# Two cached attentions in decode: aligned ring slots, and one set's query weights dealt to 64 partitions by an indirect DMA

## The chip, the cores and the metric

The kernel runs on one core of one Trainium2 chip. The metric is the device time of one execution in microseconds (us). PE is the matrix engine, DVE the vector engine, ACT the scalar engine, POOL the GpSimd engine, and SP the engine that only issues transfers here. Transfers are carried by 16 DMA engines.

## The reference, cut to what matters

One token attends to two caches of 8192 positions, one with 16 key and value heads (A), one with 8 that are shared by two query heads each (B). The two results are mixed by a gate.

```python
x = A_x                                        # [1, 1, 448]
g = sigmoid((x * gate_w).sum(-1))
q_A = (x @ A_wq).reshape(16, 256)              # B: the same, with B_wq
p_A = softmax(q_A . A_k_cache * 256 ** -0.5)   # caches: [16 or 8, 8192, 256], float32
a = (p_A @ A_v_cache).reshape(1, 4096) @ A_wo  # wo: [4096, 448]
return g * a + (1 - g) * b
```

All of it is float32. Each byte of the caches and weights is used once, so 432 MB have to come in.

## The kernel before, in words

The host lays all inputs out as one long array, `stream`, in the order of use. `plan()` cuts it into loads. A load is one `dma_start` on SP's queue: 128 partitions, `FULL` = 15,872 floats in each (63,488 bytes a partition, 8.13 MB in all), written to one of three ring slots (`SLOTS`) in SBUF. 64 loads bring the stream in; the last 13 are smaller, so that work on the last pieces can begin sooner. A load waits until the readers of what lay in its slot are done. While one load is being carried, the next is queued behind it.

There are eight sets (`NS`). A set has one B head that serves two queries and two A heads, each in four tiles of 2048 positions. Its pieces in the stream are query weights (`wq`), keys (`k`), values (`v`) and output weights (`wo`). `piece()` hands each piece to its work: `project` forms the queries of a set from `wq`, one matmul for each of seven columns of 128 input rows (columns 0 to 2 for B, 3 to 5 for A, and one for the rest of both); `spread` puts them where the scores need them; `scores` and `scores_by_row` form the scores of a tile and its probabilities `pr`, on PE and on DVE; `attend` multiplies by the values three tiles later (`LEAD`); `take`, `gather`, `combine`, `column` and `project_o` finish a head; `emit_set` multiplies by the output weights.

A `Recorder` runs `build` twice: the first pass finds which instructions others depend on, the second issues them with semaphore waits. So all instructions but a few have the line of the recorder in the profile: L184 before, L198 in the changed kernel. Tiles are told apart by name. The order of the work on each engine is that of the pieces in the stream.

The first piece of the stream, `xg`, holds the token `x` and the gate's weights; `inputs()` copies `x` into `xz`. In the code before, `xg` does not count against a load's room, so that the first load is 15,880 floats a partition, and a slot is allotted 15,936 (`SLOT`).

Of the kernel before, what the change touches and what calls it, by code (L numbers as in the profile page):

```python
# [3 lines left out]
F32 = mybir.dt.float32  # L4
# [5 lines left out]
P = 128  # L10
D = 448
DH = 256
SK = 8192
NCOL = SK // P
KF = D // P
# [19 lines left out]
TILES = [((s, r), t) for s in range(NS) for r in UNITS for t in range(NT)]  # L35

XG = 2 * (KF + 1)
SLOT = 15936
ATOM = {"half": D, "xg": XG, "k": 2 * DH, "v": 2 * DH, "wq": 2 * DH, "wo": D}  # L40

def plan():

    size = {"xg": XG, "k": ROWS * DH, "v": ROWS * DH, "wq": WQ, "wo": 8 * D}
    per = len(UNITS) * NT
    n = len(TILES)
    items = []
    for i in range(n + LEAD):
        if i == 0:  # L50
            items += [("xg", 0), ("wq", 0)]
        if i < n:
            items.append(("k", i))
        if i >= LEAD:
            items.append(("v", i - LEAD))
        if i % per == 7 and i // per + 1 < NS:
            items.append(("wq", i // per + 1))
        if i % per == LEAD + 1 and i >= per:
            items.append(("wo", i // per - 1))
    loads, room = [[]], FULL  # L60
    last = [("v", n - 3), ("v", n - 2)]
    for kind, i in items[:items.index(last[0])]:
        at, left = 0, size[kind]
        while left:
            step = min(left, room) // ATOM[kind] * ATOM[kind]
            if step:
                loads[-1].append((kind, i, at, step))
            at, left, room = at + step, left - step, room - step * (kind != "xg")
            if left:
                loads.append([])  # L70
                room = FULL

    loads = [[x] for x in loads]
    x = loads[-2][0]
    loads[-2] = [x[:2], x[2:]]
    loads[-1] += [[(kind, i, 0, size[kind])] for kind, i in last]
    at, end = 0, []
    for c in LAST_CUT:
        end.append([("v", n - 1, at, c * DH)])
        at += c * DH  # L80

    for h, n in ((3, 2), (0, 2), (1, 2)):
        end.append([("wo", NS - 1, 2 * h * D, n * D)])
    end += [[("half", c, 0, D)] for c in range(2)]
    return loads + [end]
# [137 lines left out]
        return self.rec.tile(self.name if self.psum else name, shape, dtype, bufs or self.bufs, self.psum)  # L223

def program(nc, stream, out):
    memory = {("slot", i): nc.alloc_sbuf_tensor(f"slot_{i}", [P, SLOT], F32) for i in range(SLOTS)}
    plan = Recorder(nc, memory)
    build(plan, stream, out)
    names = ["tensor", "vector", "scalar", "gpsimd"] + plan.dmas  # L230
    sems = {n: nc.alloc_semaphore(f"{n[0]}{n[1]}" if n[0] == "dma" else n) for n in names}
    rec = Recorder(nc, memory, plan.needed | {(e, plan.count[e] - 1) for e in names[:4]}, sems)
    stores = build(rec, stream, out)
    late = rec.wait("sync", [(e, rec.count[e] - 1) for e in names[:4]] + [d for d in rec.dmas if d not in stores[1:]])
    for sem, value in late:
        nc.sync.wait_ge(sem, value)
    nc.sync.sem_clear(range(sems[names[0]].num, sems[stores[1]].num))
    for d in stores[1:]:
        nc.sync.wait_ge(sems[d], 16)
    nc.sync.sem_clear(range(sems[stores[1]].num, sems[stores[-1]].num + 1))  # L240

def build(nc, stream, out):
    scale = DH ** -0.5

    const = Pool(nc, "const", 1)
# [75 lines left out]
    xz = const.tile([P, KF + 2, BLK], F32, name="xz")  # L322
    nc.vector.memset(xz, 0.0)
    gate = const.tile([1, 2], F32, name="gate")

    def clear(t, n):
        nc.tensor.matmul(t[:, :n], zero, zero[:, None, :n // 4].to_broadcast([P, 4, n // 4]), start=True, stop=False, skip_group_check=True)
# [3 lines left out]

    def inputs(xs):
        nc.vector.tensor_copy(xz[:, :KF, 0], xs[:, :KF])
        nc.vector.tensor_copy(xz[:KR, KF, 0:1], xs[:KR, KF:])
        nc.vector.tensor_copy(xz[KR:, KF + 1, 0:1], xs[KR:, KF:])

    def prepare(gw):
        clear(YY[0], D)
# [12 lines left out]

    def project(s, c0, w):

        if c0 == 0:
            QR[s] = ps_s.tile([2 * BLK, 2 * DH], F32, name="sm")
        q = QR[s]
        for j in range(w.shape[1]):
            a, c = divmod(c0 + j, KF)
            for a in (a,) if a < 2 else (0, 1):
                c = c if c0 + j < 2 * KF else KF  # L360
                nc.tensor.matmul(q[BLK * a:BLK * (a + 1), :], xz[:, c if c < KF else KF + a, :], w[:, j, :],
                                 start=(c == 0), stop=(c == KF), skip_group_check=True)
        if c0 + w.shape[1] == 2 * KF + 1:
            QR[s] = small.tile([P, NB * BLK], F32, name="px")[:2 * BLK, :2 * DH]
            nc.scalar.activation(QR[s], q, AF.Copy)
# [19 lines left out]
    def scores(u, t, j0, kt):  # L385
        M = heads(u)
        if t == 0 and j0 == 0:
            ST[u] = small.tile([P, 2, NT], F32, name="st", bufs=4)
        if j0 == 0:
            SC[u, t] = ps_sc.tile([P, NB * BLK], F32, name="sc")  # L390
        sc = SC[u, t]
        qb = QB[u[0] % 2, u[1]]
        for j in range(kt.shape[1]):
            e, g = divmod(j0 + j, NG)
            at = BLK - R[M] * g - t * M
            nc.tensor.matmul(sc[32 * g:32 * (g + 1), :], qb[:, e, at:at + 32], kt[:, j, :],
                             start=(e == 0), stop=(e == 1), skip_group_check=True)
        if j0 + kt.shape[1] < 2 * NG:
            return
        st = ST[u]  # L400
        mn = small.tile([P, 1], F32, name="mn")
        nc.vector.tensor_reduce(mn, sc, axis=AX.X, op=OP.min)
        nc.vector.tensor_tensor(st[:, 0, t:t + 1], mn, CAP[M][:, t:t + 1], op=OP.min)
        px = small.tile([P, NB * BLK], F32, name="px")
        nc.scalar.activation(px, sc, AF.Exp, bias=st[:, 0, t:t + 1], scale=-1.0, accum_out=st[:, 1, t:t + 1])
        pr = small.tile([P, NB * BLK], F32, name="pr", bufs=LEAD + 2)

        nc.vector.transpose(pr.rearrange("p (q r k) -> p q k r", r=BLK, k=2),
                            px.rearrange("p (q k c) -> p q k c", c=BLK, k=2))
        PR[u, t] = pr.rearrange("p (q c) -> p q c", c=2 * BLK)  # L410

    def scores_by_row(u, t, j0, kt):

        if t == 0 and j0 == 0:
            ST[u] = small.tile([P, 2, NT], F32, name="st", bufs=4)
        st = ST[u]
        n = kt.shape[1]
        nc.vector.tensor_tensor(kt, kt, QA[u][:, None, :].to_broadcast([P, n, DH]), op=OP.mult)
        if j0 == 0:
            SC[u, t] = small.tile([P, ROWS], F32, name="sr")  # L420
        sc = SC[u, t]
        nc.vector.tensor_reduce(sc[:, j0:j0 + n], kt, axis=AX.X, op=OP.add)
        if j0 + n < ROWS:
            return
        mn = small.tile([P, 1], F32, name="mn")
        nc.vector.tensor_reduce(mn, sc, axis=AX.X, op=OP.min)
        mt = small.tile([P, BLK], F32, name="mt")
        nc.vector.transpose(mt, mn.to_broadcast([P, BLK]))
        nc.vector.tensor_reduce(st[:, 0, t:t + 1], mt, axis=AX.X, op=OP.min)
        px = small.tile([P, ROWS // 2, 2], F32, name="pxr")  # L430
        nc.scalar.activation(px.rearrange("p q k -> p (q k)"), sc, AF.Exp, bias=st[:, 0, t:t + 1], scale=-1.0,
                             accum_out=st[:, 1, t:t + 1])
        pr = small.tile([P, NB * BLK], F32, name="pr", bufs=LEAD + 2)[:, :ROWS * NG * NT].rearrange(
            "p (q c k) -> p q c k", c=NG * NT, k=2)
        nc.vector.tensor_tensor(
            pr, px[:, :, None, :].to_broadcast([P, ROWS // 2, NG * NT, 2]),
            cols[:, t].rearrange("p g r -> p (g r)")[:, None, :, None].to_broadcast([P, ROWS // 2, NG * NT, 2]), op=OP.mult)
        PR[u, t] = pr.rearrange("p q c k -> p q (c k)")
# [13 lines left out]
    def take(u):  # L452

        o = O.pop(u)
        ob1 = small.tile([P, DH], F32, name="ob1", bufs=1)
        OB[u] = small.tile([P, DH], F32, name="ob", bufs=3)
        nc.scalar.activation(ob1, o[:, DH:], AF.Copy, scale=half[:, 1:2])
        nc.vector.scalar_tensor_tensor(OB[u], o[:, :DH], half[:, 0:1], ob1, op0=OP.mult, op1=OP.add)

# [14 lines left out]
    def combine(u):  # L474
# [14 lines left out]
        nc.vector.tensor_reduce(z[:, :M], es.rearrange("p (c m) -> p m c", m=M), axis=AX.X, op=OP.add)  # L489
        rz = small.tile([1, 2], F32, name="rz")  # L490
        nc.vector.reciprocal(rz[:, :M], z[:, :M])
        WR[u] = small.tile([1, NG // M, n, M, 2], F32, name=f"wr{M}")
        for m in range(M):
            nc.vector.tensor_scalar(
                WR[u][:, :, :, m, :], ew[:, None, m::M, None].to_broadcast([1, NG // M, n, 2]),
# [83 lines left out]
    def piece(kind, i, at, view):  # L579
        n = view.shape[-1] // ATOM[kind]  # L580
        j0 = at // ATOM[kind]
        if kind == "xg":
            inputs(view[:, :KF + 1])
            GW[0] = view[:, KF + 1:]
        elif kind == "wq":
            project(i, j0, view.rearrange("p (c n) -> p c n", c=n))
            if j0 + n < 2 * KF + 1:
# [39 lines left out]

    off = 0
    for fill in LOADS:
        buf = ring.tile([P, SLOT], F32, name="slot")  # L630
        c = 0
        for load in fill:
            n = sum(x[3] for x in load)
# [76 lines left out]
```

## Time and profile before

| | us |
|---|---|
| median of 3 runs (lowest, highest) | 1009.67 (1009.52, 1009.75) |
| the profiled execution | 1009.6 |
| its span, first to last instruction | 1007.9 |
| PE busy | 579.3 (57%) |
| DVE busy | 458.8 (46%) |
| ACT busy | 94.4 (9%) |
| read from HBM | 432.02 MB, 429 GB/s over the span |
| chain that ended last: share of DMA | 75% |

The times of the steps below come from the one profiled execution. It lies 0.07 us under the median, and 1.7 us of it lie outside the span. In windows of time, the DMA share is the mean busy share of the 16 DMA engines: 0.50 would be eight of them at work. The chain of work follows the end back to whatever released each step.

### The profile page before, as it was taken

The page shows a single profiled execution, that of the slowest core. Times are in us where ns is not written, and L with a number is a line of the kernel's source. Part 1 is how long each engine was busy: PE and PEld are TensorE (multiplying, and loading weights), DVE is VectorE, ACT ScalarE, POOL GpSimd, SP SyncE. Part 2 cuts the span into 40 slices and gives each one's busy share as a digit, 9 for nine tenths or more (in the row PEclk, how much of TensorE's full clock was granted, in tenths as well). Part 3 has the DMA queues.
Part 4 walks back from the last instruction along what each step waited for, and adds up shares of the span by engine and source line. Part 5 has one row for each costly group of instructions (what it writes and reads, how often), then busy time and mean ns, then how long its engine had stood idle before and what let it go on. Part 6 is the DMA issues. An engine that isn't in the chain of part 4 may idle for free.

```text
span 1007.9 us, 7387 instructions
## 1 busy us (share of the span) xinstructions
PE 579.3 (57%) x3154; PEld 170.5 (17%) x3154; DVE 458.8 (46%) x644; ACT 94.4 (9%) x308; POOL 1.9 (0%) x10
## 2 busy tenths in 40 slices
PE   0755745565755655646645475655645637636557
PEld 0211211121211111112111121111211112101112
DVE  1386213961248521576214851248521585215851
ACT  0100100010100110001100000100110101101011
POOL 0000000000000000000000000000000000000000
PEclk9877777767777877787877867876976777777788
DMA  9999999999999999999999999999999999999997
GB/s 403 442 433 421 437 439 434 431 429 434 437 437 423 431 437 438 426 431 434 437 431 434 428 437 431 437 424 438 431 437 431 434 428 437 434 433 421 441 413 328
DMA packets 9256, 432.48 MB, mean 429 GB/s; under 512 B 1032, under 2 KB 1288, under 8 KB 1928
## 3 DMA queue, kind: packets, MB, share of 16 engines
q1 hardware_dynamic: 9220, 432.02, 99.3%
q8 instruction: 24, 0.39, 0.2%
q14 instruction: 8, 0.07, 0.0%
q10 hardware_dynamic: 4, 0.00, 0.0%
HBM read 432.02 MB, written 0.00 MB: 429 GB/s over the span
## 4 chain that ended last, share of the span: by engine, by line
DMA 75%; PE 13%; DVE 11%; ACT 1%; issue 0%; SPq 0%
DMA slot<-in_stream_dram 75%; PE ps_o L184 6%; PE ps_sc L184 5%; DVE sr L184 4%; DVE slot L184 4%; PE ps_s L184 1%; DVE pr L184 1%; DVE mn L184 1%; ACT px L184 0%; PE ps_y L184 0%; ACT pxr L184 0%; DVE st L184 0%; DVE ob L184 0%; ACT ew L184 0%; DVE mt L184 0%
## 5 line engine op out<-in xcount | busy, mean ns | idle before, releaser
L184 PE MATMUL ps_o<-slot,pr 128*32 128x512 f32 (+1 forms) x1536 | 352.0, 760 | 227.2 <-DMA slot<-in_stream_dram 227.2
L184 PE MATMUL ps_sc<-slot,qb 128*32 128x512 f32 x1024 | 195.9, 715 | 105.1 <-DMA slot<-in_stream_dram 105.0
L184 DVE TENSOR_REDUCE mn<-ps_sc 128x1 f32<-128x512 f32 x64 | 44.1, 690 | 338.5 <-PE ps_sc L184 308.3
L184 DVE TENSOR_TENSOR slot<-slot,qa 128x4096 f32<-128x4096 f32 (+7 forms) x40 | 142.6, 3565 | 42.7 <-DMA slot<-in_stream_dram 42.6
L184 PEld LDWEIGHTS ps_o<-slot,pr 128*32 128x32 f32 (+1 forms) x1536 | 80.2, 142 | 408.4 <-DMA slot<-in_stream_dram 255.7
L184 DVE TENSOR_REDUCE sr<-slot 128x16 f32<-128x4096 f32 (+7 forms) x40 | 142.7, 3567 | 1.4
L184 PEld LDWEIGHTS ps_sc<-slot,qb 128*32 128x32 f32 x1024 | 46.6, 130 | 222.9 <-issue 129.4
L184 ACT ACTIVATE px<-ps_sc,st 128x512 f32<-128x512 f32 x64 | 44.0, 688 | 408.2 <-DVE st L184 408.2
L184 DVE STREAM_TRANSPOSE pr<-px 128x512 f32<-128x512 f32 x64 | 45.7, 714 | 54.1 <-ACT px L184 54.1
L184 PE MATMUL ps_s<-slot,xz 128*32 128x512 f32 (+1 forms) x136 | 45.6, 664 | 34.9 <-DVE xz L184 22.9
L184 ACT ACTIVATE pxr<-sr,st 128x16 f32<-128x16 f32 x32 | 9.9, 308 | 372.9 <-DVE st L184 372.9
L184 PE MATMUL ps_s<-sel,ob 128*128 128x1 f32 (+1 forms) x96 | 18.4, 296 | 37.7 <-DVE ob L184 37.7
L184 DVE SCALAR_TENSOR_TENSOR ob<-ps_o,half,ob 128x256 f32<-128x256 f32 x24 | 11.3, 473 | 45.9 <-ACT ob L184 45.9
L184 PEld LDWEIGHTS ps_s<-sel,ob 128*128 128x128 f32 x96 | 16.3, 239 | 62.5 <-DVE ob L184 54.2
L184 PEld LDWEIGHTS ps_s<-slot,xz 128*32 128x32 f32 (+1 forms) x136 | 11.4, 125 | 63.9 <-issue 27.2
L184 DVE TENSOR_TENSOR pr<-pxr,cols 128x256 f32<-128x256 f32 x32 | 13.6, 425 | 15.0 <-ACT pxr L184 15.0
L184 PE MATMUL ps_y<-slot,ocs 128*1 128x448 f32 (+1 forms) x176 | 15.8, 476 | 0.0
L184 ACT ACTIVATE ob<-ps_o,half 128x256 f32<-128x256 f32 x24 | 11.3, 470 | 43.6 <-PE ps_o L184 43.5
L184 PE MATMUL ps_s<-px,spread 64*128 64x256 f32 x16 | 7.1, 532 | 13.9 <-DVE es L184 13.9
L184 PE MATMUL ps_s<-ones,wr 1*128 1x1 f32 x48 | 9.5, 264 | 6.5 <-DVE wr L184 6.5
L184 ACT ACTIVATION_READ_ACCUMULATOR px<-ps_sc,st 128x1 f32 x64 | 12.3, 193 | 0.0
L184 PEld LDWEIGHTS ps_s<-ones,wr 1*128 1x128 f32 x48 | 7.4, 193 | 28.2 <-DVE wr L184 13.3
(62 smaller groups left out, 137.0 us busy)
## 6 DMA issues: line engine op xcount, KB each, us to landing
slot<-in_stream_dram SPq DMA_DIRECT2D x50, 7936.0 KB, 43.0
slot<-in_stream_dram SPq DMA_DIRECT2D x1, 7940.0 KB, 21.8
slot<-in_stream_dram SPq DMA_DIRECT2D x1, 4864.0 KB, 41.4
slot<-in_stream_dram SPq DMA_DIRECT2D x2, 2048.0 KB, 33.3
slot<-in_stream_dram SPq DMA_DIRECT2D x1, 3072.0 KB, 37.8
slot<-in_stream_dram SPq DMA_DIRECT2D x3, 448.0 KB, 33.2
slot<-in_stream_dram SPq DMA_DIRECT2D x1, 1280.0 KB, 31.7
slot<-in_stream_dram SPq DMA_DIRECT2D x1, 1024.0 KB, 32.2
```

Source lines behind the costliest of these rows:

```text
L184: i = getattr(e, what)(*args, **kw)
```

## The change: what it does

Slots are allotted 15,872 floats each behind a tile `pad`, whose length is worked out from the first free byte so that it comes out as a multiple of 256. In the program as built, the first slot began at byte 4224 of a partition before (16 times 256, and 128 over); with the change it begins at byte 1312 (5 times 256, and 32 over), since the pad itself is placed at byte 1152, and a slot is 248 times 256 bytes long.

Columns 0 to 2 of set 2's `wq` (384 rows of 512 floats, 786,432 bytes) leave the stream. The host lays them out as an array `dealt` of 64 rows of 3072 floats (12,288 bytes), each of six of the 384 rows. An indirect DMA, which POOL issues, puts row `row[p]` of it in partition p of a new tile `dq`; for the 64 partitions that get none, `row[p]` is out of bounds and nothing is written. Which partitions get a row is set by the table `DEAL`: partitions are grouped in 16 groups of eight by the DMA engine that is meant to serve them, and `DEAL` says how many of a group's eight get a row. Eight groups get 8, 8, 8, 8, 8, 8, 7 and 6, three get 1, and five get none. `xg` grows by `row` and by the matching values of `x` (`dx`), and counts against the room now. In `project`, set 2 begins with six matmuls on `dq` in the place of three on the slot.

To make room in SBUF, `pr` has four buffers in the place of five, `ob` two in the place of three, `wr1` and `wr2` one each in the place of two, and the scratch for POOL's transfers is 1 KB a partition in the place of 4 KB.

```diff
-XG = 2 * (KF + 1)
-SLOT = 15936
+DEAL = {0: 8, 2: 1, 3: 6, 4: 1, 5: 8, 6: 7, 7: 8, 8: 8, 9: 1, 10: 8, 15: 8}
+NR = sum(DEAL.values())
+DN = KF * P // NR
+DS = 2
+DX = 2 * (KF + 1)
+XG = DX + 8
...
+def dealt_partitions():
+
+    groups = {}
+    for p in range(P):
+        groups.setdefault(8 * (p // 64) + p // 4 % 8, []).append(p)
+    return sorted(p for g, n in DEAL.items() for p in groups[g][:n])
...
+        if (kind, i) == ("wq", DS):
+            at, left = KF * 2 * DH, left - KF * 2 * DH
...
-            at, left, room = at + step, left - step, room - step * (kind != "xg")
+            at, left, room = at + step, left - step, room - step
...
-    memory = {("slot", i): nc.alloc_sbuf_tensor(f"slot_{i}", [P, SLOT], F32) for i in range(SLOTS)}
+    nc.alloc_sbuf_tensor("pad", [P, -nc.sbuf_base % 256 // 4], F32)
+    memory = {("slot", i): nc.alloc_sbuf_tensor(f"slot_{i}", [P, FULL], F32) for i in range(SLOTS)}
...
+    dq = const.tile([P, DN, 2 * DH], F32, name="dq")
+    nc.gpsimd.memset(dq, 0.0)
+    row = const.tile([P, 1], mybir.dt.uint32, name="row")
+    dx = const.tile([P, DN - 1 + BLK], F32, name="dx")
+    nc.vector.memset(dx, 0.0)
...
+        nc.vector.tensor_copy(row, xs[:, DX:DX + 1])
+        nc.vector.tensor_copy(dx[:, :DN], xs[:, DX + 1:DX + 1 + DN])
+        nc.gpsimd.indirect_dma_start(dq.rearrange("p j n -> p (j n)"), None, dealt,
+                                     bass.IndirectOffsetOnAxis(ap=row, axis=0), bounds_check=NR - 1, oob_is_err=False)
...
+        if s == DS and c0 == KF:
+            for j in range(DN):
+                k = DN - 1 - j
+                n = BLK if j == 0 else 1
+                nc.tensor.matmul(q[:n, :], dx[:, k:k + n], dq[:, k, :], start=(j == 0), stop=False, skip_group_check=True)
...
-        pr = small.tile([P, NB * BLK], F32, name="pr", bufs=LEAD + 2)
+        pr = small.tile([P, NB * BLK], F32, name="pr", bufs=LEAD + 1)
...
-        OB[u] = small.tile([P, DH], F32, name="ob", bufs=3)
+        OB[u] = small.tile([P, DH], F32, name="ob")
...
-        WR[u] = small.tile([1, NG // M, n, M, 2], F32, name=f"wr{M}")
+        WR[u] = small.tile([1, NG // M, n, M, 2], F32, name=f"wr{M}", bufs=1)
...
-    nc = _bacc.Bacc("TRN2", target_bir_lowering=False, num_devices=1, dynamic_dma_scratch_size=4096)
+    nc = _bacc.Bacc("TRN2", target_bir_lowering=False, num_devices=1, dynamic_dma_scratch_size=1024)
```

On POOL the new work stands behind the set-up of the program. Its last rows before, with the engine whose semaphore each waits for, are these:

```order
L184 IOTA pos_0 128x32
L184 IOTA pos_0 128x16
L184 IOTA px 128x128 x2
L184 IOTA rows_0 128x4
L184 IOTA px 128x128 [waits vector]
```

And with the change:

```order
L198 IOTA px 128x128 x2
L198 IOTA rows_0 128x4
L198 IOTA px 128x128 [waits vector]
L198 MEMSET dq 128x3072
L198 DMA dq<-in_dealt_dram,row 128x3072 [waits gpsimd,vector]
```

The clearing of `dq` and the indirect DMA are the last that POOL does; the DMA waits for DVE's copy of `row`, which comes in with the first load.

On PE the other end of it stands where set 2's queries are formed, between the first `attend` of an A head of set 1 (`ps_o`, 32x512) and the next scores (`ps_sc`). Before:

```order
L184 MATMUL ps_s<-sel,ob 128x2 x2
L184 MATMUL ps_o<-slot,pr 32x512 x8
L184 MATMUL ps_s<-slot,xz 32x512 x8
L184 MATMUL ps_sc<-slot,qb_0 32x512 x8
L184 MATMUL ps_s<-gs_0,ones 1x32
```

With the change:

```order
L198 MATMUL ps_s<-sel,ob 128x2 x2
L198 MATMUL ps_o<-slot,pr 32x512 x8
L198 MATMUL ps_s<-dq,dx 32x512
L198 MATMUL ps_s<-dq,dx 1x512 x5
L198 MATMUL ps_s<-slot,xz 32x512 x5
L198 MATMUL ps_sc<-slot,qb_0 32x512 x8
L198 MATMUL ps_s<-gs_0,ones 1x32
```

Three of the eight matmuls on the slot are gone, and six on `dq` stand ahead of the other five.

On DVE the fewer buffers of `pr` show in the tiles that are scored by row: the write of `pr` gets a second wait, for PE's `attend` of four tiles before. The first such tile of the program, before:

```order
L184 TENSOR_REDUCE sr<-slot 128x16 [waits vector]
L184 TENSOR_REDUCE mn<-sr 128x1 [waits vector]
L184 STREAM_TRANSPOSE mt<-mn 128x32 [waits vector]
L184 TENSOR_REDUCE st<-mt 128x1 [waits vector]
L184 TENSOR_TENSOR pr<-pxr,cols 128x256 [waits scalar]
```

With the change:

```order
L198 TENSOR_REDUCE sr<-slot 128x16 [waits vector]
L198 TENSOR_REDUCE mn<-sr 128x1 [waits vector]
L198 STREAM_TRANSPOSE mt<-mn 128x32 [waits vector]
L198 TENSOR_REDUCE st<-mt 128x1 [waits vector]
L198 TENSOR_TENSOR pr<-pxr,cols 128x256 [waits scalar,tensor]
```

23 of the 32 such writes have this second wait now, and none had it before. The stream still comes in 64 loads, and set 2's pieces and all that follow stand 1,536 floats a partition earlier in it.

More of the change, by code (lines that the diff above doesn't have):

```diff
@@ L223, in tile, with program @@
         return self.rec.tile(self.name if self.psum else name, shape, dtype, bufs or self.bufs, self.psum)
-def program(nc, stream, out):
-    memory = {("slot", i): nc.alloc_sbuf_tensor(f"slot_{i}", [P, SLOT], F32) for i in range(SLOTS)}
+def program(nc, stream, dealt, out):
+    nc.alloc_sbuf_tensor("pad", [P, -nc.sbuf_base % 256 // 4], F32)
+    memory = {("slot", i): nc.alloc_sbuf_tensor(f"slot_{i}", [P, FULL], F32) for i in range(SLOTS)}
     plan = Recorder(nc, memory)
-    build(plan, stream, out)
+    build(plan, stream, dealt, out)
     names = ["tensor", "vector", "scalar", "gpsimd"] + plan.dmas
@@ L232, in program @@
     rec = Recorder(nc, memory, plan.needed | {(e, plan.count[e] - 1) for e in names[:4]}, sems)
-    stores = build(rec, stream, out)
+    stores = build(rec, stream, dealt, out)
     late = rec.wait("sync", [(e, rec.count[e] - 1) for e in names[:4]] + [d for d in rec.dmas if d not in stores[1:]])
@@ L240, in program, with build @@
     nc.sync.sem_clear(range(sems[stores[1]].num, sems[stores[-1]].num + 1))
-def build(nc, stream, out):
+def build(nc, stream, dealt, out):
     scale = DH ** -0.5
@@ L333, in inputs @@
         nc.vector.tensor_copy(xz[:, :KF, 0], xs[:, :KF])
-        nc.vector.tensor_copy(xz[:KR, KF, 0:1], xs[:KR, KF:])
-        nc.vector.tensor_copy(xz[KR:, KF + 1, 0:1], xs[KR:, KF:])
+        nc.vector.tensor_copy(xz[:KR, KF, 0:1], xs[:KR, KF:KF + 1])
+        nc.vector.tensor_copy(xz[KR:, KF + 1, 0:1], xs[KR:, KF:KF + 1])
+        nc.vector.tensor_copy(row, xs[:, DX:DX + 1])
+        nc.vector.tensor_copy(dx[:, :DN], xs[:, DX + 1:DX + 1 + DN])
+        nc.gpsimd.indirect_dma_start(dq.rearrange("p j n -> p (j n)"), None, dealt,
+                                     bass.IndirectOffsetOnAxis(ap=row, axis=0), bounds_check=NR - 1, oob_is_err=False)
     def prepare(gw):
@@ L352, in project @@
     def project(s, c0, w):
-        if c0 == 0:
+        if s not in QR:
             QR[s] = ps_s.tile([2 * BLK, 2 * DH], F32, name="sm")
         q = QR[s]
+        if s == DS and c0 == KF:
[3 more added lines that the diff above has]
+                nc.tensor.matmul(q[:n, :], dx[:, k:k + n], dq[:, k, :], start=(j == 0), stop=False, skip_group_check=True)
         for j in range(w.shape[1]):
@@ L432, in scores_by_row @@
                              accum_out=st[:, 1, t:t + 1])
-        pr = small.tile([P, NB * BLK], F32, name="pr", bufs=LEAD + 2)[:, :ROWS * NG * NT].rearrange(
+        pr = small.tile([P, NB * BLK], F32, name="pr", bufs=LEAD + 1)[:, :ROWS * NG * NT].rearrange(
             "p (q c k) -> p q c k", c=NG * NT, k=2)
@@ L582, in piece @@
         if kind == "xg":
-            inputs(view[:, :KF + 1])
-            GW[0] = view[:, KF + 1:]
+            inputs(view)
+            GW[0] = view[:, KF + 1:DX]
         elif kind == "wq":
@@ L629, in build @@
     for fill in LOADS:
-        buf = ring.tile([P, SLOT], F32, name="slot")
+        buf = ring.tile([P, FULL], F32, name="slot")
         c = 0
@@ L690 @@
     parts["half"] = halves(parts["wo"][NS - 1][:, 4 * D:6 * D])
-    parts["xg"] = [_np.concatenate([col(get("A_x")), col(get("gate_w"))], axis=1)]
+    at = dealt_partitions()
+    b = parts["wq"][DS].reshape(P, -1, 2 * DH)[:, :KF].transpose(1, 0, 2).reshape(NR, DN, 2 * DH)
+    x = _np.zeros((P, 1 + DN), _np.float32)
+    x[:, 0] = NR
+    x[at, 0] = _np.arange(NR)
+    x[at, 1:] = get("A_x").reshape(D)[:KF * P].reshape(NR, DN)
+    parts["xg"] = [_np.concatenate([col(get("A_x")), col(get("gate_w")), x, x[:, :XG - DX - 1 - DN] * 0], axis=1)]
     laid = {
@@ L695 @@
             for fill in LOADS for load in fill]),
+        "dealt": b.reshape(NR, -1),
     }
-    nc = _bacc.Bacc("TRN2", target_bir_lowering=False, num_devices=1, dynamic_dma_scratch_size=4096)
+    nc = _bacc.Bacc("TRN2", target_bir_lowering=False, num_devices=1, dynamic_dma_scratch_size=1024)
     arrays, args = {}, []
```

## The prediction

> **What bounds the kernel now.** I read the page's table of slices and its DMA part first, then short windows at the end of the run, then the chain of work.
>
> ```profile
> span 1007.9 us, 7387 instructions
> PE 579.3 (57%) x3154; PEld 170.5 (17%) x3154; DVE 458.8 (46%) x644; ACT 94.4 (9%) x308; POOL 1.9 (0%) x10
> DMA  9999999999999999999999999999999999999997
> q1 hardware_dynamic: 9220, 432.02, 99.3%
> q8 instruction: 24, 0.39, 0.2%
> q14 instruction: 8, 0.07, 0.0%
> DMA slot<-in_stream_dram 75%; PE ps_o L184 6%; PE ps_sc L184 5%; DVE sr L184 4%; DVE slot L184 4%; PE ps_s L184 1%; DVE pr L184 1%; DVE mn L184 1%; ACT px L184 0%; PE ps_y L184 0%; ACT pxr L184 0%; DVE st L184 0%; DVE ob L184 0%; ACT ew L184 0%; DVE mt L184 0%
> ```
>
> The DMA engines are full in every slice but the last, and the stream (q1) takes 99.3% of their time: the bytes bound the kernel, not an engine's work. Beside the stream run only fetches of instructions (q8, q14), 32 packets. The last slice holds the rest of the answer, so it is opened (window, us, busy time of PE, PEld, DVE, ACT, POOL, granted clock, DMA share, GB/s):
>
> ```profile
> 1.60:998.00 996.40, 573.12 (x3070) 167.80 (x3070) 457.43 (x639) 92.44 (x304) 0.92 (x3) 0.77 1.00 432
> 999.00:999.50 0.50, 0.50 (x8) 0.00 (x0) 0.00 (x0) 0.00 (x0) 0.00 (x0) 1.00 1.04 405
> 999.50:1000.00 0.50, 0.29 (x6) 0.14 (x4) 0.00 (x0) 0.00 (x0) 0.00 (x0) 1.00 0.89 344
> 1000.00:1000.50 0.50, 0.50 (x4) 0.00 (x0) 0.00 (x0) 0.00 (x0) 0.00 (x0) 1.00 0.79 314
> 1000.50:1001.00 0.50, 0.30 (x3) 0.01 (x2) 0.00 (x0) 0.00 (x0) 0.00 (x0) 1.00 0.66 265
> 1001.00:1002.00 1.00, 1.00 (x4) 0.14 (x4) 0.00 (x0) 0.00 (x0) 0.00 (x0) 1.00 0.59 240
> 1002.00:1003.00 1.00, 0.04 (x2) 0.00 (x0) 0.40 (x1) 0.47 (x1) 0.00 (x0) 1.00 0.58 237
> 1003.00:1004.00 1.00, 0.86 (x19) 0.84 (x20) 0.09 (x1) 0.17 (x1) 0.00 (x0) 1.00 0.56 219
> 1004.00:1004.50 0.50, 0.50 (x32) 0.47 (x24) 0.00 (x0) 0.00 (x0) 0.00 (x0) 1.00 0.48 183
> 1004.50:1005.00 0.50, 0.50 (x28) 0.43 (x18) 0.00 (x0) 0.00 (x0) 0.00 (x0) 1.00 0.12 47
> ```
>
> The share falls to 0.56-0.59 by 1001 us, stays there for three microseconds, and then goes. 0.56 of 16 is nine. So the 16 engines do not end together: seven end around 1000.3 us (16 x 0.5 us x the shares above 0.56 from 999.5 to 1001, and 0.03 of the next, give seven engines 0.8 us on average after 999.5), nine around 1004.5 (16 x 0.5 us x (0.48 + 0.12) = 4.8 us, over nine engines 0.53 us after 1004.0), the last near 1004.9. All carry the same bytes of the stream, and until then all are busy. What sets nine back is the only other traffic: 9 x 4.2 us = 38 us over 32 fetches, 1.2 us each, though their 0.46 MB are 17 us at the rate worked out below, 0.53 us each. A fetch so costs an engine some 0.66 us beyond its bytes. A load has landed when the slowest engine has delivered its part, so the end goes by the latest of the nine.
>
> The chain of work (start, us, what) shows the pace and the tail:
>
> ```profile
> 588.70 36.48 DMA slot<-in_stream_dram
> ...
> 749.23 46.23 DMA slot<-in_stream_dram
> ...
> 811.43 40.27 DMA slot<-in_stream_dram
> ...
> 968.27 32.68 DMA slot<-in_stream_dram
> ...
> 1000.99 1.08 PE ps_o L184 x4
> ...
> 1003.77 2.19 PE ps_y L184 x64
> ...
> 1005.98 0.28 DVE ys L184
> ```
>
> Landings at 795.46 and 851.70 are 56.24 us apart. That is three loads of 8.126 MB (two or four would be 289 or 578 GB/s, against 432 in the windows): 18.75 us a load, 433 GB/s, 27.1 GB/s an engine. The last piece that the chain waits for lands at 1000.95; the matmuls of the last output weights end about a microsecond after the last bytes. Since every late landing goes by the slowest engine, a shift of that engine shifts them all, and this tail with them.
>
> **The change, part by part.**
>
> *Less in the stream.* 786,432 bytes over 16 engines are 49,152 an engine, at 27.1 GB/s 1.81 us less on each, the late ones too: -1.81. `xg` adds 32 bytes a partition, nothing to speak of.
>
> *The dealt rows.* A row is 12,288 bytes, 0.454 us at an engine's rate. That is the lower price. The upper one is that of the nearest row, a fetch of instructions of 8 or 16 KB out of another queue: 0.454 + 0.66 = 1.11 us. Eight rows of one queue come together here, while fetches come singly, so I take the bytes' price, and keep the other as a rival. [...]
>
> Who gets the rows decides. `DEAL` gives no more than one row to eight engines, and 6, 7 or 8 rows to the other eight. The windows show nine late engines. Nine and eight are seventeen: if the fetches fall as before, at least one late engine gets 6 or more. The fetches should fall as before, since they can only follow the count of instructions: on PE 24 fetches of q8 for 6,308 matmuls and weight loads, one in 263, and the change adds some 12 there and some 26 on DVE, copies, a clearing and waits. [...]
>
> The late engine is on average 0.4 us ahead of the last (1004.53 against 1004.9). With 61/8 = 7.6 rows, the mean of the eight full groups, it ends at -0.4 - 1.81 + 7.6 x 0.454 = +1.24 us against the last engine of before. The other late ones end at -1.81 or -1.36. The seven early ones end at most at -4.6 + 0.9 + 8 x 0.454 - 1.81 = -1.9 (latest of them near 1001.2). So the sum of the rows is +1.24, from 0 (6 rows, the earliest late engine, 0.9 us ahead) to +1.8 (8 rows, the last engine); with the cost of one fetch on top once, +2.5.
>
> *Six matmuls for three, the copies, the clearing.*
>
> ```profile
> L184 PE MATMUL ps_s<-slot,xz 128*32 128x512 f32 (+1 forms) x136 | 45.6, 664 | 34.9 <-DVE xz L184 22.9
> L184 DVE COPY xz<-slot x3: 139/151/169, 22.6 to 22.9; 64x1 f32<-64x1 f32 x2, 128x3 f32<-128x3 f32 x1
> L184 POOL IOTA px<- 128x128 f32 x3 | 1.3, 458 | 0.9 <-DVE half L184 0.9
> ```
>
> Eight sets of eight matmuls (two passes each) and the gate's four are the 136, so three more are six passes of 0.66 us, +4.0 us on PE at set 2. Two copies of 0.15 us and a small clearing are on DVE near 23 us. On POOL the clearing of 3,072 columns is bounded by the row of 128 columns (0.458 us, 24 times that is 11 us) and by nothing; it starts near 3.4 us, ahead of the first landing, and the DMA behind it is POOL's last. `dq` is wanted by PE in set 2, over 100 us later (a set is about 120 us). All of it costs the end nothing as long as loads are queued early enough: in the chain a load was issued 36.48 us before it landed at the least before the tail, of which 18.75 are its own, so it could have come 17.7 us later, and still 13 where an engine is 4.6 us ahead.
>
> *Fewer buffers.* Each of 23 writes of `pr` on DVE now waits for an `attend` of four tiles before:
>
> ```profile
> L184 DVE TENSOR_TENSOR slot<-slot,qa 128x4096 f32<-128x4096 f32 (+7 forms) x40 | 142.6, 3565 | 42.7 <-DMA slot<-in_stream_dram 42.6
> L184 DVE TENSOR_REDUCE sr<-slot 128x16 f32<-128x4096 f32 (+7 forms) x40 | 142.7, 3567 | 1.4
> L184 PE MATMUL ps_o<-slot,pr 128*32 128x512 f32 (+1 forms) x1536 | 352.0, 760 | 227.2 <-DMA slot<-in_stream_dram 227.2
> ```
>
> Those values land ahead of the keys, DVE works 8.9 us on a tile's keys (285.3 us over 32 tiles) before it writes, and PE needs 352.0/96 = 3.7 us for an `attend`: it is done by then. Were DVE held, its release of the slot would be what is late, within the 13 us above. Price nothing.
>
> *The slots' start.* If the start costs nothing, as I take it, the term is 0. The built slots begin 32 bytes past a multiple of 256, so what the pad is named for does not come about.
>
> The sum: 1009.67 + 1.24 = 1010.9 us.
>
> **The rivals.**
>
> 1. *The deal fits.* If the ninth late engine is not late in the changed program (another engine carries its fetches, or shares them), the end goes by late engines with no row (-1.81) or one (-1.36 if it is one of the last): 1009.67 - 1.6 = 1008.1. For it: the eight lightly dealt groups agree in number with nine less one. Against: 0.56 to 0.59 of 16 is nine, not eight (0.50).
>
> 2. *Each dealt row costs like a fetch* (slower). At 1.11 us a row, early engines end at -4.6 - 1.81 + 8 x 1.11 = +2.5, 1012.1 us, and a late one with 7.6 rows at -0.4 - 1.81 + 8.4 = +6.2, 1015.9 us. It decides where a row costs over (1.81 + 4.6)/8 = 0.80 us, whoever gets them. For it: 38 us of lateness against 17 us of bytes; against: the rows come in one lot.
>
> 3. *The slots' start pays.* A row of 63,488 bytes is 248 blocks of 256 bytes and takes 18.75/8 = 2.34 us. If a start off the multiple costs a 249th block, that is 9.4 ns, over 432.02 MB / 16 / 63,488 = 425 rows 4.0 us: 1004.1 with the first rival, 1006.9 with the sum. For it: the rate of 27.1 GB/s is steady, as a limit would be. Against: 32 bytes over is as much off as 128. [...]
>
> 4. *Nothing shows*: rows on a mildly late engine cancel the 1.81; 1009.7.
>
> **How the numbers follow.** A measurement of this kernel can tell about 0.2%, 2.0 us, from no change. The forecast (1010.9; own range 1009.7 to 1012.2) gets 0.36; the first rival (1007.8 to 1008.7) 0.27; the second (1011.5 to 1016) 0.19; the third 0.09; the fourth 0.09. The range leaves out the third (0.09) and the second above 1013.3 (0.10): 1007.5 to 1013.3. Faster by over 0.2% (under 1007.65): the third and a fifth of the first, 0.09 + 0.05 = 0.14. Slower by over 0.2% (over 1011.69): the second but for its low end, 0.17, and a quarter of the forecast, 0.09: 0.26. Within 0.2%: the remaining 0.60.
>
> **What would show it.** In windows of the last 6 us of the changed kernel: under the forecast the share goes low, to one or two engines of 16 (0.06 to 0.13) for a microsecond or more at the end, after most have stopped together; under the first rival it falls from 1 to 0 within about 1.5 us; under the second the full groups are last, a share of 0.5 for two microseconds and more. The load's pace tells the third: landings in the chain three loads apart would be 56.0 us, not 56.24. A wait of PE for `dq`, or loads issued less than 24 us before landing, would say that the cover I named is gone. The number of q8 and q14 packets tells whether the fetches moved. I am wrong if the share before is not a count of engines (one engine could be busy half the time), or if a row's engine is not the one that `DEAL` means.

## The result, and the profile after

| | before | after |
|---|---|---|
| median of 15 runs, us (lowest, highest) | 1009.77 (1009.43, 1010.18) | 1011.76 (1011.64, 1012.95) |
| ratio to before (95% interval) | | 1.0020 (1.0012 to 1.0028) |
| the profiled execution, us | 1009.6 | 1011.84 |
| its span, us | 1007.9 | 1010.2 |

The change makes the kernel 2.0 us slower, 0.2%. The forecast was 1010.9 us (+1.24), in the range 1007.5 to 1013.3. As the experiments show, the rows cost 1.15 to 1.26 us, where 1.24 were forecast for them, and the start of the slots, which was priced at nothing, another 0.75 us.

From the page of the changed kernel, its totals, the table of slices and the queues:

```profile
span 1010.2 us, 7424 instructions
PE 591.6 (59%) x3160; PEld 171.7 (17%) x3160; DVE 461.2 (46%) x647; ACT 94.2 (9%) x308; POOL 5.7 (1%) x12
DMA  9999999999999999999999999999999999999997
q1 hardware_dynamic: 9220, 431.24, 99.0%
q0 software_dynamic: 144, 0.79, 0.2%
q8 instruction: 24, 0.39, 0.2%
q14 instruction: 8, 0.07, 0.0%
```

The DMA engines are as full as before. The stream is 0.78 MB less, the dealt rows (q0) are the same bytes over again, and the fetches of instructions are 24 and 8 as before. So the engines carry the same bytes and the end still comes later. The windows at the end (window, us, busy time of PE, PEld, DVE, ACT, POOL, granted clock, DMA share, GB/s) show how:

```profile
1001.00:1002.00 1.00, 0.81 (x10) 0.14 (x4) 0.00 (x0) 0.00 (x0) 0.00 (x0) 1.00 0.82 320
1002.00:1003.00 1.00, 0.86 (x4) 0.00 (x0) 0.00 (x0) 0.00 (x0) 0.00 (x0) 1.00 0.67 257
1003.00:1004.00 1.00, 0.93 (x4) 0.14 (x4) 0.00 (x0) 0.00 (x0) 0.00 (x0) 1.00 0.52 195
1004.00:1005.00 1.00, 0.12 (x2) 0.00 (x0) 0.33 (x1) 0.47 (x1) 0.00 (x0) 1.00 0.26 100
1005.00:1006.00 1.00, 0.79 (x16) 0.78 (x20) 0.16 (x1) 0.12 (x1) 0.00 (x0) 1.00 0.25 95
1006.00:1007.00 1.00, 1.00 (x48) 0.78 (x36) 0.00 (x0) 0.05 (x1) 0.00 (x0) 1.00 0.19 72
1007.00:1008.00 1.00, 0.97 (x22) 0.54 (x16) 0.00 (x0) 0.26 (x1) 0.00 (x0) 1.00 0.01 2
```

Before, nine engines (0.56) worked to the end and stopped together. Now a share of 0.25 to 0.26, four engines of 16, works on alone from 1004 to beyond 1006. The chain of work (start, us, what) holds the difference too: the last piece that it waits for landed at 1000.95 before and lands at 970.92 + 32.10 = 1003.02 now, 2.07 us later.

```profile
218.05 33.40 DMA slot<-in_stream_dram
...
617.01 48.69 DMA slot<-in_stream_dram
...
813.56 40.62 DMA slot<-in_stream_dram
864.31 46.14 DMA slot<-in_stream_dram
...
970.92 32.10 DMA slot<-in_stream_dram
```

Two landings three loads apart, at 854.18 and 910.45, are 56.27 us apart, against 56.24 before.

### The profile page after: what moved, and what is told of

Its sections match the earlier page's. It is cut to its first block, busy times and chain, and to the rows that moved or that the text cites. A ratio compares the mean times of both kernels' runs of the same rounds, so it can differ in the third digit from the quotient of the medians.

```text
span 1010.2 us, 7424 instructions
## 1 busy us (share of the span) xinstructions
PE 591.6 (59%) x3160; PEld 171.7 (17%) x3160; DVE 461.2 (46%) x647; ACT 94.2 (9%) x308; POOL 5.7 (1%) x12
## 3 DMA queue, kind: packets, MB, share of 16 engines
q1 hardware_dynamic: 9220, 431.24, 99.0%
## 4 chain that ended last, share of the span: by engine, by line
DMA 70%; DVE 17%; PE 12%; ACT 1%; issue 1%; SPq 0%; DVEq 0%
DMA slot<-in_stream_dram 70%; DVE sr L198 7%; DVE slot L198 7%; PE ps_sc L198 5%; PE ps_o L198 5%; PE ps_s L198 1%; DVE pr L198 1%; DVE mn L198 1%; ACT pxr L198 0%; ACT px L198 0%; DVE wr L198 0%; ACT ew L198 0%; DVE st L198 0%; PE ps_y L198 0%; DVE mt L198 0%
## 5 line engine op out<-in xcount | busy, mean ns | idle before, releaser
L198 PE MATMUL ps_sc<-slot,qb 128*32 128x512 f32 x1024 | 198.9, 744 | 94.3 <-DMA slot<-in_stream_dram 94.2
L198 PE MATMUL ps_s<-slot,xz 128*32 128x512 f32 (+1 forms) x130 | 41.0, 638 | 27.5 <-DVE xz L198 22.1
```

The lines of the kernel that those rows point to most:

```text
L198: i = getattr(e, what)(*args, **kw)
```

## The experiments

Each kernel differs from the changed one by the edit shown (e7 from the kernel before), and those with an interval were timed against the kernel before on the same chip. Its medians there were 1009.62 to 1009.88, and e1 to e4 ran on one chip, e5 to e8 on a second, e9 and e10 on a third, so that a difference of up to 0.3 us between runs of two chips can be the chips'. Two questions were open: what the dealt rows cost, and what the start of the slots costs. The results, by both:

| slots begin, over a multiple of 256 | nothing dealt, us | dealt as by the change, us | dealt by a table that spares the late engines, us |
|---|---|---|---|
| 128 bytes | 1009.8 (before) | 1011.01 (e8) | |
| 32 bytes | 1010.61 (e1) | 1011.76 (after) | 1009.17 (e9) |
| none | 1007.64 (e6), 1007.75 (e7) | 1008.88 (e2) | 1006.17 (e10) |

### No deal, and the start on a true multiple (e1, e2)

e1 puts the three columns back in the stream; the slots' start and the smaller numbers of buffers stay as changed. The tile `dq`, the copies and the indirect DMA are gone.

```diff
-DS = 2
+DS = -1
```

> All of set 2's query weights are back in the stream; the slots start at byte 1312 as in the changed kernel, and the fewer buffers are kept. Theory (full groups of the deal hold engines that the fetches set back): the last landing and the time fall back to those of before, 1009.8 us, with nine engines late at the end (a DMA share of 0.56 for three microseconds). Rival (the slots' new start costs): it stays at 1010.2 or above, by what the start costs. Rival (the dealt rows cost more than their bytes): as the theory.

Measured: 1010.61 us (1010.53 to 1010.70), ratio 1.0007 (0.9998 to 1.0016). So the deal, with all its copies and matmuls, is 1011.76 - 1010.61 = 1.15 us of the loss (1.26 with each taken against the kernel before on its own chip), and the rest is there without it, as the first rival said. In the windows the nine engines are back for the last microseconds:

```profile
1002.00:1003.00 1.00, 0.86 (x6) 0.00 (x0) 0.00 (x0) 0.09 (x1) 0.00 (x0) 1.00 0.59 229
1003.00:1004.00 1.00, 0.05 (x1) 0.05 (x1) 0.48 (x1) 0.38 (x1) 0.00 (x0) 1.00 0.57 224
1004.00:1005.00 1.00, 1.00 (x25) 0.95 (x29) 0.00 (x0) 0.17 (x1) 0.00 (x0) 1.00 0.58 219
1005.00:1006.00 1.00, 1.00 (x40) 0.74 (x31) 0.00 (x0) 0.00 (x0) 0.00 (x0) 1.00 0.22 77
```

e2 keeps the deal and gives the pad 32 floats, so that the slots begin at byte 1280.

```diff
-    nc.alloc_sbuf_tensor("pad", [P, -nc.sbuf_base % 256 // 4], F32)
+    nc.alloc_sbuf_tensor("pad", [P, 32], F32)
```

> Only the pad differs from the changed kernel: 32 floats, so that the slots start at byte 1280, a true multiple of 256. If a start off the multiple costs a 249th block for each row, 4.0 us are saved: 1007.8 us, and loads in the chain are 56.0 us apart by threes. If only the new 32 bytes over cost (the rows' median packet and the pace seem some 0.007 us a load slower than before), 0.4 us: 1011.4 us. If the start is of no account: 1011.8 us. The theory on the deal says nothing on it.

Measured: 1008.88 us (1008.82 to 1009.01), ratio 0.9990 (0.9981 to 0.9999), 2.88 us faster than the changed kernel, between the prices that were named (4.0 and 0.4). The start counts.

### The same number of rows for every engine (e3)

```diff
-DEAL = {0: 8, 2: 1, 3: 6, 4: 1, 5: 8, 6: 7, 7: 8, 8: 8, 9: 1, 10: 8, 15: 8}
+DEAL = {g: 4 for g in range(16)}
```

> The table gives every group of eight partitions four rows. Theory: each engine gets back the 1.81 us that the stream lost, so nine engines are late as before and the end is where it was: 1009.8 us (up to 1010.3 if the slots' start costs). Rival (each row costs like a fetch, 1.11 us in the place of 0.454): 4 x 0.66 = 2.6 us more, 1012.4 us. Rival (a group's rows are not carried by one engine of its own): no change against the changed kernel is told apart by this run alone; then it stays at 1011.8 us.

Measured: 1010.65 us (1010.48 to 1011.78), ratio 1.0009 (1.0000 to 1.0018): what the kernel without a deal takes (1010.61). Four rows cost each engine what 1.81 us less of the stream gave it, so a row is (1.81 + 0.04)/4 = 0.46 us, its bytes and nothing more. The end has the same shape as without the deal:

```profile
1002.00:1003.00 1.00, 0.80 (x4) 0.00 (x0) 0.00 (x0) 0.15 (x1) 0.00 (x0) 1.00 0.58 226
1003.00:1004.00 1.00, 0.11 (x1) 0.11 (x1) 0.48 (x1) 0.32 (x1) 0.00 (x0) 1.00 0.57 222
1004.00:1005.00 1.00, 1.00 (x28) 0.95 (x32) 0.00 (x0) 0.17 (x1) 0.00 (x0) 1.00 0.58 219
1005.00:1006.00 1.00, 1.00 (x42) 0.75 (x32) 0.00 (x0) 0.00 (x0) 0.00 (x0) 1.00 0.20 72
```

So the 1.15 us lie in who gets the rows.

### Which engines are late (e4, e5)

Two tables that give each group a pair of numbers of its own, 0, 2, 6 or 8 rows in each.

```diff
-DEAL = {0: 8, 2: 1, 3: 6, 4: 1, 5: 8, 6: 7, 7: 8, 8: 8, 9: 1, 10: 8, 15: 8}
+DEAL = {g: (0, 2, 6, 8)[g // 4] for g in range(16)}     # e4
+DEAL = {g: (0, 2, 6, 8)[g % 4] for g in range(16)}      # e5
```

> A probe for which engines are set back: groups 0 to 3 get no row, 4 to 7 two, 8 to 11 six, 12 to 15 eight. Theory: rows cost 0.46 us, so the engines fall into four classes of +0, +0.9, +2.8 and +3.7 us after the deal, and the end shows in which class the latest engine is; the time is 1010.8 to 1012.3 us if one of the engines with many fetches is in groups 12 to 15, 1009.9 to 1011.0 us if the latest is in groups 8 to 11 alone. Rival (rows cost like a fetch): classes of +0, +2.2, +6.7 and +8.9 us, and 1013 us or more.

> The second probe: a group g gets 0, 2, 6 or 8 rows by g modulo 4. With the first probe, the pair of counts names the group of an engine that is set back, if the fetches fall on the same engines in both. Theory: rows cost 0.46 us and the time is 1010.6 plus what the latest engine has over its share: -1.8 + 0.46 n us, 1010.6 to 1012.5 us. Rival (fetches fall on other engines in each program): the pairs contradict the changed kernel's own counts, and the table cannot be set by them.

Measured: 1012.37 us, both, one execution each; e4 is 0.07 us above the range expected for it, e5 within its own. The trace keeps the queue, size, start and duration of each packet, but not its engine. While the engines are full, the next packet of an engine starts some 4 ns before the record of the last one ends, so the packets can be followed in 16 chains, one for each engine; where two chains meet within a few nanoseconds, they can be taken for one another. In e3 each of the 16 chains holds four dealt rows. Setting the packets of 12,288 bytes of each chain beside its fetches, in e4, e5 and the changed kernel, tells which group meets which fetches. The 24 fetches of PE (q8) fall on eight groups in turn, 5, 6, 9, 10, 11, 12, 13 and 14, three each. Of q14's eight, five are DVE's (they are 127 to 129 of its instructions apart in the kernel before), all on group 3; two on group 1 are taken for ACT's (123 of its instructions apart there), and the last is on group 4. By the time from the row ahead of a fetch to the rows behind it, one for PE sets its engine back about 1.5 us, one for DVE about 1.0, and ACT's two together 1.3. That makes nine late engines: 3, 5, 6 and 9 to 14. The last windows check this list. Of e4:

```profile
1004.00:1005.00 1.00, 0.71 (x4) 0.00 (x0) 0.00 (x0) 0.24 (x1) 0.00 (x0) 1.00 0.41 160
1005.00:1006.00 1.00, 0.20 (x2) 0.20 (x2) 0.48 (x1) 0.23 (x1) 0.00 (x0) 1.00 0.38 142
1006.00:1007.00 1.00, 1.00 (x32) 0.95 (x35) 0.00 (x0) 0.17 (x1) 0.00 (x0) 1.00 0.22 81
```

And of e5:

```profile
1005.00:1006.00 1.00, 0.23 (x2) 0.23 (x2) 0.48 (x1) 0.20 (x1) 0.00 (x0) 1.00 0.33 124
1006.00:1007.00 1.00, 1.00 (x32) 0.95 (x35) 0.00 (x0) 0.17 (x1) 0.00 (x0) 1.00 0.14 54
```

By the list, in e4 the late groups 12, 13 and 14 have eight rows and 9, 10 and 11 six: six engines near the end (6/16 = 0.38), then three (0.19). In e5 3 and 11 have eight, and 6, 10 and 14 six: five (0.31), then two (0.13). The shares are 0.38 and 0.22, 0.33 and 0.14. And in the changed kernel four of the late ones, 3, 5, 6 and 10, have 6 to 8 rows: 4/16 = 0.25, against 0.25 and 0.26.

### Start and deal apart from each other (e6, e7, e8)

e6 is e1 with e2's pad; e7 is the kernel before with a pad of 32 floats ahead of the slots, which then begin at byte 4352; e8 is the changed kernel with a pad of 64 floats, whose slots begin at byte 1408, 128 over a multiple, as those of before do.

```diff
+    nc.alloc_sbuf_tensor("pad", [P, 32], F32)     # e6 (with DS = -1), e7
+    nc.alloc_sbuf_tensor("pad", [P, 64], F32)     # e8
```

> No deal, and the slots start on a true multiple of 256. If start and deal add up, the start's saving is as in the changed kernel, 2.9 us: 1010.6 - 2.9 = 1007.7 us. If the saving hung on the dealt rows, it stays at 1010.6.

> The kernel before with a pad of 32 floats alone: slots start at byte 4352, a multiple of 256, in the place of 4224, 128 over. Theory (a start off the multiple costs each row of 63,488 bytes some 6 ns, as the paces of the traces say: 18.749 against 18.701 us a load): 53 x 0.048 = 2.5 us saved, 1007.3 us. A 249th block would be 4.0 us: 1005.8 us. If the kernel without the deal is slower than before for its fewer buffers and not for its start, 1007.0 us or less here and 1007.7 us there.

> The changed kernel with a pad of 64 floats: slots start at byte 1408, 128 over as before, in the place of 32 over. If the 0.8 us by which the kernel without the deal is slower than before are the start's, they are saved: 1011.0 us. If they are the fewer buffers' or the first load's, it stays at 1011.8 us.

Measured: e6 1007.64 us (1007.52 to 1008.03), ratio 0.9978 (0.9969 to 0.9987); e7 1007.75 (1007.61 to 1008.03), 0.9979 (0.9970 to 0.9988); e8 1011.01 (1010.91 to 1011.13), 1.0011 (1.0002 to 1.0020).

From a start 128 bytes over to a multiple the gain is 2.10 us (before to e7) and 2.13 (e8 to e2); from 32 over it is 2.97 (e1 to e6) and 2.88 (after to e2). So 32 over costs 0.75 us more than 128 over (e8 to after). On a multiple the deal costs 1008.88 - 1007.64 = 1.24, against 1.15 (1.21 against 1.26, with each run taken against the kernel before on its own chip): the two causes add up. e7 saved less than the 2.5 us expected for it. e6 and e7 differ by 0.11: the fewer buffers cost nothing that shows.

Where a start is paid is seen in the chain, in rows that e2 and e8 have in common. First e2, on a multiple, then e8, 128 over:

```profile
168.90 43.59 DMA slot<-in_stream_dram
...
615.45 48.79 DMA slot<-in_stream_dram
...
861.88 46.27 DMA slot<-in_stream_dram
...
968.35 31.91 DMA slot<-in_stream_dram
```

```profile
168.32 44.40 DMA slot<-in_stream_dram
...
616.79 48.74 DMA slot<-in_stream_dram
...
863.82 46.26 DMA slot<-in_stream_dram
...
970.42 32.01 DMA slot<-in_stream_dram
```

e8's landings are later by 0.23 us at 212, 1.29 at 665, 1.93 at 910 and 2.17 at 1002: not a step at one place but every load a little, while the engines are full. Those of the changed kernel, 32 over, are later still than e8's, by 0.17 us at 665, 0.37 at 910 and 0.59 at 1003. The pad moves the tiles behind the slots as well; that the stream's rows pay is seen in their packets. Along the chains of packets, one row of 63,488 bytes starts 2338.9 ns after the other on the mean in e2, 2342.4 in e8 and 2343.7 in the changed kernel. Over some 425 such rows an engine, the 3.5 and 4.8 ns are 1.5 and 2.0 us. A fetch of PE sets its engine back 1.42 us in e2 and 1.55 in the other two, another 0.4 us over three. That leaves 0.2 of the 2.1 us and 0.5 of the 2.9 us without a place.

### The deal on the engines that are early (e9, e10)

```diff
-DEAL = {0: 8, 2: 1, 3: 6, 4: 1, 5: 8, 6: 7, 7: 8, 8: 8, 9: 1, 10: 8, 15: 8}
+DEAL = {0: 8, 1: 8, 2: 8, 3: 1, 4: 8, 5: 1, 6: 1, 7: 8, 8: 8, 9: 1, 10: 1, 11: 1, 12: 1, 14: 1, 15: 8}
```

e10 has e2's pad as well.

> As the changed kernel (slots still begin 32 bytes past a multiple of 256), with another table: the seven groups whose engines carry no instruction fetches of PE or DVE (0, 1, 2, 4, 7, 8, 15) get 8 rows each, and eight of the nine others one each. Theory 1 (a row costs its engine only its bytes, about 0.455 us, and the end is set by the engines that the fetches set back): each late engine loses 49,152 bytes of stream, 1.81 us, and gets 0.455 back at most, so the end comes 1.35 us before that of the kernel without the deal (1010.61): 1009.3, and the share of the DMA engines at the end falls from about 0.5 to nothing within 1.5 us, with no part at 0.26. Theory 2 (the rows, or the packets for skipped rows, or the fewer buffers hold something up wherever they are): 1011 to 1012, like the changed kernel's 1011.76.

> The same table, and a pad of 32 floats, so that the first slot begins at byte 1280, a multiple of 256. If the two causes are independent and add up: the kernel without the deal and with this start (1007.64) less 1.35 = 1006.3; a load's period of about 18.70 us. If the start and the deal act on the same wait, one gain swallows the other: about 1007.6.

Measured: e9 1009.17 us (1008.98 to 1009.27), ratio 0.9995 (0.9986 to 1.0004), where 1009.3 was expected and the rival said 1011 to 1012. e10 1006.17 (five of six runs from 1006.10 to 1006.47, and one 1008.99), ratio 0.9967 (0.9954 to 0.9979), where 1006.3 was expected. So the same 64 rows are worth 1.4 to 1.5 us against no deal by the medians (1010.61 to 1009.17, and 1007.64 to 1006.17), or 1.2 with each run taken against the kernel before on its own chip, and with the start 3.4 us against the kernel before. The end of e9:

```profile
1001.00:1002.00 1.00, 0.51 (x4) 0.00 (x0) 0.00 (x0) 0.44 (x1) 0.00 (x0) 1.00 1.01 391
1002.00:1003.00 1.00, 0.40 (x4) 0.40 (x4) 0.48 (x1) 0.03 (x1) 0.00 (x0) 1.00 0.84 319
1003.00:1004.00 1.00, 1.00 (x38) 0.91 (x42) 0.00 (x0) 0.17 (x1) 0.00 (x0) 1.00 0.55 201
1004.00:1005.00 1.00, 0.98 (x32) 0.50 (x21) 0.00 (x0) 0.00 (x0) 0.00 (x0) 1.00 0.06 22
```

All 16 engines work until 1002 and nearly all stop within two microseconds. That seven groups can have eight rows and end no later than the others bears the list above out. So do the chains of e9: those with PE's fetches or DVE's hold one row at most, and the other seven hold eight each. These seven groups have 56 partitions, so that eight of the 64 rows had to go to late engines; fewer and longer rows were not tried.

## Why the prediction was right, and where it was not

**Less in the stream, -1.81: right.** e3 gives it and takes it back with four rows an engine, to 0.04 us.

**The price of a row: right at its lower end.** 0.46 us measured, 0.454 taken. The second rival (1.11 us a row) is out: with four rows an engine it would have put e3 at 1010.61 - 1.81 + 4.4 = 1013.2, and e3 took 1010.65. In the trace rows of q0 and of q1 alternate on an engine one by one, and a dealt row's packet takes 0.46 us there too. That the turns are free is what e3 adds: 1010.65 us with four of them an engine, against 1010.61 with none. A fetch costs more beyond its bytes than the 0.66 us reckoned: one of PE's has 0.60 us of bytes and sets its engine back 1.55.

**Who gets the rows, +1.24: right in size, short in number.** The argument from nine and eight said that at least one late engine has 6 rows or more. There are four. The end goes by the latest engine alone, so three more beside it cost nothing: the deal measured 1.15 to 1.26 us. That the mean of the rows over the mean of the late engines came so near is in part luck, since which late engine held how many rows was not known, and the term's bounds were 0 and 1.8. But the mark that was named, a share of one or two engines at the end (0.06 to 0.13), was wrong; the share was 0.25. The prediction named it as a way to be wrong that a row's engine might not be the one that `DEAL` means; e4, e5 and e9 show that it is: the list worked out from the groups gave shares of 0.38 and 0.19 for e4, 0.31 and 0.13 for e5, against 0.38 and 0.22, 0.33 and 0.14 in the windows, and e9, dealt by that list, took 1009.17 us. The first rival, a deal that fits, is out for this table, and e9 is what it would have been: 1009.17 on this start, 1.2 to 1.4 us under no deal, where the rival reckoned 1.6 under the kernel before.

**Matmuls, copies, clearing, buffers, 0: right.** The six matmuls and the clearing took this (count, then shortest, median and longest ns, and first and last start):

```profile
L198 PE MATMUL ps_s<-dq,dx x12: 592/593/1061, 217.4 to 223.1; 128*1 128x512 f32 x10, 128*32 128x512 f32 x2
L198 POOL MEMSET dq<- x1: 2657/2657/2657, 3.4 to 3.4; 128x3072 f32 x1
```

No row shows PE waiting for `dq`. The load that was issued latest before its landing, ahead of the tail, was issued at 218.05, where these matmuls start, 33.40 us ahead: 3.1 us less cover than the least before (36.48), against the 4 us reckoned for PE there. The 33.40 are still 14.7 more than a load's own 18.75, so nothing of it reached the end. The clearing's 2.7 us lie near the lower of its bounds.

**The slots' start, 0: this step failed.** It is the term that was mis-sized: the built start, 32 bytes over, costs 0.75 us more than that of before, 128 over, and both cost against a multiple, 2.9 and 2.1 us. The step took it, without a reason, that a start off the multiple costs nothing, and the third rival held that "32 bytes over is as much off as 128"; e1 against before on its chip (+0.73) and e8 against after (-0.75) contradict both. The third rival had the shape, a cost on each row of 63,488 bytes, but the change does not collect it, since its own pad comes out 32 bytes wrong; where a kernel does (e2, e6, e7, e10), the price is 2.1 to 3.0 us, with 3.5 to 4.8 ns on each row. The 249th block, 9.4 ns a row and 4.0 us in all, is not what the runs show. Why a start off the multiple costs at all, and why 32 over costs more than 128, stays open.

The sum as measured: deal +1.2, start +0.75, together 1.95 of 1.99 us. The 1011.76 lie 0.07 over the bound that the prediction drew for slower by over 0.2%, and the interval of the ratio has that bound inside, so by these runs the change is slower, and whether by more or by less than 0.2% is not settled.

## What to carry to other kernels

Where the DMA engines are full from start to end, open the last microseconds: the share times 16 counted the engines that were still at work (nine, six and five here), and the ones that stopped early can be given more bytes, but only once it is known which ones they are; a table of the wrong engines (1011.76) is worse than an even one (1010.65), and the right one is better than both (1009.17). Find them with a probe that marks each group with a number of its own, not from a count that happens to agree. And read the address at which a buffer was really placed: a pad that is worked out from the first free byte missed its multiple by 32 bytes, which cost 2.9 us in 1009.

## What the runs showed of the hardware that was not expected

Fetches of instructions ride on the engines that carry the data, and not evenly: PE's 24 go to eight engines in turn, and DVE's to one, so that nine of 16 end some four microseconds late (a share of 0.56 to 0.59 in the windows of before). Each of PE's puts the stream on its engine back about 1.5 us, and in this kernel, which the bytes bound (the stream takes 99% of the DMA engines' time), that is what the end waits for. Whether PE waits for a fetch no run here shows.

The start of a tile in SBUF moves the time of this stream by 0.2 to 0.3%, with loads of 63,488 bytes a partition: 3.5 ns on a row of 2.34 us for 128 bytes over a multiple of 256, 4.8 for 32 over, and 0.13 us on a fetch of PE.

The 64 rows left 144 packets on q0: 64 of the rows, 16 of four bytes, as each of the 64 loads has beside its 128 rows (64 x 144 of q1's 9,220), and 64 more of four bytes, as many as there are partitions that get no row. The four-byte ones took 9 ns each in the changed kernel, and at e3's price of a row they cost nothing that shows.
